# Exponentials drawn together ahead of a sine, and a later place for the values' loads and sums

## The chip, the cores and the metric

The kernel runs on one core of a Trainium2 chip. A core has five engines with their own instruction queues: TensorE (PE, whose weight loads are listed as PEld), VectorE (DVE), ScalarE (ACT), GpSimd (POOL) and SyncE (SP), which here issues almost all DMA transfers. Each engine works through its queue in order and waits at semaphores for the others. The metric is the device time of one execution in microseconds (us); lower is better. A single execution with the hardware profiler gives the trace; its times are counted from the first instruction of the span.

## The reference

An attention with pooled keys and values is followed by a two-layer network with a snake activation, all in float32:

```python
B, H, S, D = 8, 8, 576, 64
k_p = k.reshape(B, H, S // 8, 8, D).mean(axis=3)      # 72 pooled keys per head
v_p = v.reshape(B, H, S // 8, 8, D).mean(axis=3)
scores = np.matmul(q, k_p.transpose(0, 1, 3, 2)) / np.sqrt(D)
attn = np.exp(scores - np.max(scores, axis=-1, keepdims=True))
attn = attn / (np.sum(attn, axis=-1, keepdims=True) + 1e-09)
x = np.matmul(attn, v_p)              # -> (4608, 512), heads side by side
h = x @ w_in                          # 512 -> 2048
s = np.sin(alpha * h)
g = h + s * s / (alpha + 1e-09)
out = g @ w_out                       # 2048 -> 512
```

## The kernel before

The network's first layer runs over the 4608 rows in nine units of 512 (`u` = 0 to 8), and each unit in four groups (`J` = 0 to 3) of the 2048 columns. The products use a scheme of seven block products in place of eight, so a group consists of seven products. They are the seven steps `k` = 0 to 6 of a group, and a unit thus has 28 *slots* (slot = 7 J + k). `hidden` writes this order out by hand. For each slot it records the copies, sines and squares of the group on ScalarE, the additions on VectorE, then whatever is listed for the slot in `extra`, and then the slot's product on TensorE (L833). Since every engine works through its queue in the order of recording, the slot of a piece of work fixes what it stands behind.

`carry` makes the list `extra` of each unit. While unit `u` is multiplied, the attention of batch `b = u + 1` is worked in between, for the 512 rows that the next unit needs. Its steps, with their lines in the profile, are these:
- `load_v` (L141, L146): six DMA transfers on SP bring the values into the tiles `kvin` (two of 512 KB) and `vr` (four of 64 KB). `pool_main` adds the values of `kvin` up into `vm` on GpSimd in three additions (L132), and `pool_v` those of `vr` into `vz` in four (L132 and L152).
- `load_k` (L122), twice per unit: each call brings 576 KB of the keys of the batch after the next into a `kvin` tile; `pool_k` adds each up on GpSimd (L132) into `kp`. The `kvin` tiles come from a pool of two buffers, so that the three loads of a unit take turns: the second key load uses the buffer that the unit's values were in.
- `load_q` (L85, L106): the queries of the unit after the next.
- `two_scores` (L309 on TensorE, L332 and L333 on VectorE): the scores of four row tiles, less their maximum, into `ex`.
- `exp` (L358, ScalarE) on each of the four tiles, 128x864 the last one and 128x576 the others; `norm`: sum and reciprocal on VectorE (L364, L365), then the multiplication by it on GpSimd (L366), called the division here.
- `turn` (L492 to L502): block transposes on VectorE into the tile `tr`; `move` (L512): 16 DMA transfers on SP from `tr` into `aM`.
- `all_values` (L601, L614): the products with the values, and the copies (L528) that write the next unit's rows.
- `turn_q` (L220, L225 on VectorE, L235 on SP): the queries are transposed in the same way, through the same buffer `tr`, and moved.

Four things of `hidden` matter beside these. In steps 1 and 3 of a group ScalarE copies one PSUM bank into another (L811) before the next product may add to it. In step 4 the group's first sine comes (L980), followed by its square (L987). Groups 1 to 3 of the units 1 to 6 take one product from seven smaller ones (L962; group 3 a second one, L1010); their raw results are copied by ScalarE (L967) and added on GpSimd (L795, five additions, the *raw sums*, recorded in step 2). And the finished `g` of a group is written to DRAM by SP (`store_g`, L1046).

Sine and exponential need different function tables on ScalarE: where one follows the other, the program has a table load (ACT_TABLE_LOAD).

The units 1 to 6 are those that run the part of `carry` that the diff touches; unit 6 has no keys and no queries to load any more. When unit 8 is done, the second layer (L1310) runs alone to the end.

In the code of `hidden` the extras of step 4 stand behind the sine and the square:

```python
            elif k == 4:
                ...
                    sin(G, 0, 0, G.b1)
                    square(G, 0, 0)
                extras()
                ...
                product(G, 7, G.b7, part=(0, 1))
```

Of the kernel before, what the change touches and what calls it, by code (L numbers as in the profile page):

```python
# [41 lines left out]
class Kernel:  # L42
# [1107 lines left out]
    def carry(self, u):  # L1150

        nc = self.nc
        x = defaultdict(list)
        at = lambda slot, f, *a: x[slot].append(lambda: f(*a))
        last = self.B - 1
        b = u + 1
        if u == 0:
            A0, A = self.att[:2]
            at(1, self.sum_v_rows, 0, 1, 2)
            at(1, A0.rest_q)  # L1160
            at(1, A0.a_head, 1, (5, 7, 2))
            at(2, A0.values, (2, 3), (2, 1), 1, 1)
            at(2, A0.score, 4)
            at(2, self.sums_of_x, 0, 2)
            at(2, self.sums_of_x, 0, 3)
            at(2, self.load_w_in_part, 2)
            at(2, self.load_w_in_part, 3)
            at(2, self.pairs_q, 1, range(5))
            at(4, self.combine_w_in, 1, (0, 1, 2, 3), self.nc.gpsimd)
            at(4, A.q_t, 0, self.nc.vector.tensor_copy)  # L1170
            at(4, A.q_t, 1, self.nc.vector.tensor_copy)
            at(4, A.k_t)
            at(7, self.load_v, 1)
            at(7, lambda: self.pool_main())
            at(7, lambda: self.pool_v())
            for i in range(2):
                at((5, 10)[i], A.two_scores, i)
            at(13, A.two_shifts)
            for i in range(2, 5):
                at(5 + i, A.q_t, i)  # L1180
            at(9, A0.exp, 4)
            for i in range(4):
                at((9, 9, 15, 15)[i], A.exp, i)
                at((10, 10, 16, 16)[i], A.norm, i)
                at((13, 13, 17, 19)[i], A.turn, i)
            at(8, self.combine_w_in, 2, (0, 1, 2, 3), self.nc.gpsimd)
            at(13, A0.norm_rest)
            at(17, self.combine_w_in, 3, (0, 1), self.nc.gpsimd)
            at(17, self.combine_w_in, 3, (2, 3), self.nc.gpsimd)
            at(23, A0.a_rest)  # L1190
            at(24, lambda: A0.values_rest((5, 6, 7, (self.turn + 1) % 5)))
            for r in (32, 96):
                at(3, self.nc.gpsimd.memset, self.aM[r:r + 32, :, 704:736], 0.0)
            at(19, A.move, range(3))
            at(20, A.move, (3,), nc.scalar, (0,))
            at(21, A.move, (3,), nc.scalar, (1,))
            at(26, A.all_values)
            at(9, self.load_q, 2)
            at(23, self.inner_w_in)
            for e in range(2):  # L1200
                at(12, self.load_k, 2, e)
                at(17, lambda e=e: self.pool_k[e]())
            at(27, self.att[2].k_t)
            turn = 23
        else:
            at(0, self.sums_of_x, u, 2)
            at(0, self.sums_of_x, u, 3)
        if 0 < u < last:
            A = self.att[b]
            for i in range(2):  # L1210
                at((3, 5)[i], A.two_scores, i)
            at(6, A.two_shifts)
            for i in range(4):
                at((8, 10, 10, 11)[i], A.exp, i)
                at((9, 10, 11, 12)[i], A.norm, i)
                at((12, 13, 13, 13)[i], A.turn, i)
            at(14, A.move, range(4))
            at(2, self.load_v, b)
            at(5, lambda: self.pool_main())
            at(6, lambda: self.pool_v())  # L1220
            for i in range(2):
                if b < last:
                    at(12, self.load_k, b + 1, i)
                    at(17, lambda i=i: self.pool_k[i]())
            at(25, A.all_values)
            if b < last:
                at(26, self.att[b + 1].k_t)
            if 2 < u + 2 <= last:
                at(7, self.load_q, u + 2)
            at(2, self.inner_x, u)  # L1230
            turn = 22
        elif u:
            turn = None
        if turn and u + 2 <= last:
            for part in range(4):
                at(((turn, turn + 1) if u == 0 else (23, 24))[part] if part < 2 else turn + part, self.turn_q, u + 2, part)
        if u + 1 < self.NU:
            at(27, self.sums_of_x, u + 1, 0)
            at(27, self.sums_of_x, u + 1, 1)
        return x  # L1240
# [337 lines left out]
```

## Time and profile before

| | |
|---|---|
| median of 3 runs | 922.52 us (920.09 to 923.7) |
| the profiled execution | 925.12 us |
| its span, first to last instruction | 923.3 us |
| granted TensorE clock, mean | 0.998 |
| first layer with attention, about | 0 to 528 us |
| one unit with attention, e.g. from the first scores of u=2 to those of u=3 | 150.35 to 207.66 us: 57.3 us |
| second layer alone | from 558 us to the end |
| ACT_TABLE_LOAD | 31 x 1283 ns |

The lines of the trace read as: start in us, duration in us, engine, source line, operation, the tile written and the tile read with their sizes, how many instructions were merged into the line (x2), and in brackets the idle time of the engine before it with what ended that idle time. An engine that is busy all the time can be sped up only by taking work from it; one that waits shows in the brackets for whom. For TensorE the weight loads (PEld) run ahead of the products, so a wait shows there first and a little longer.

### The profile page before, as it was taken

Reading aid. Unit: us, or ns where it says so; the run is one execution under the profiler, and the core shown is the slowest. Engines: PE = TensorE matmul, PEld = TensorE weight load, DVE = VectorE, ACT = ScalarE, POOL = GpSimd, SP = SyncE. Lnnn points to the kernel's source line nnn. Section 1 sums busy time; section 2 is a strip of 40 time slices with the busy share of each in tenths; the row PEclk is TensorE's granted clock in tenths of the full one; section 3 lists DMA queues with packets and bytes.
Section 4 is the critical chain, followed back from the end, with each engine's and each line's share of the span. In section 5 each row is a group of like instructions: output and inputs, shape, how many; then the busy total and the mean of one; then the engine's idle time right before and its main releaser. Section 6 shows DMA issues by size and latency. Waiting matters only on the chain.

```text
span 923.3 us, 18073 instructions
## 1 busy us (share of the span) xinstructions
PE 901.2 (98%) x7050; PEld 816.9 (88%) x7050; DVE 670.0 (73%) x999; ACT 462.3 (50%) x1064; POOL 264.4 (29%) x306
## 2 busy tenths in 40 slices
PE   8999999999999989999999999999999999999998
PEld 5787878788787878878888899999999999999998
DVE  7685766656566555764466989988888897989795
ACT  5686776977859758687786631111111211111111
POOL 4688663755637647463000000000000000000000
PEclk9999999999999999999999999999999999999999
DMA  9965847658466565637526237161526353443501
GB/s 255 242 195 159 244 121 204 173 155 258 127 192 180 155 208 154 169 108 212 217 92 207 103 124 222 36 219 39 181 77 170 89 159 99 135 123 99 158 15 39
DMA packets 128748, 141.14 MB, mean 153 GB/s; under 512 B 46920, under 2 KB 95704, under 8 KB 128664
## 3 DMA queue, kind: packets, MB, share of 16 engines
q1 hardware_dynamic: 125880, 137.88, 51.2%
q10 hardware_dynamic: 2784, 2.11, 0.9%
q8 instruction: 56, 0.92, 0.5%
q14 instruction: 28, 0.23, 0.1%
HBM read 75.37 MB, written 47.19 MB: 133 GB/s over the span
## 4 chain that ended last, share of the span: by engine, by line
PE 86%; ACT 10%; DVE 2%; issue 1%; POOL 1%; DVEq 0%; POOLq 0%
PE PS L1310 40%; PE PS L833 36%; PE PS L309 2%; ACT s L980 2%; PE PS L601 2%; ACT L980 2%; ACT L358 2%; ACT ex L358 2%; ACT s L987 1%; PE PS L962 1%; PE PS L1010 1%; PE PS L614 1%; ACT PS L811 1%; ACT raw L967 1%; DVE x L1265 1%
## 5 line engine op out<-in xcount | busy, mean ns | idle before, releaser
L833 PE MATMUL PS<-home,a 128*128 128x256 f32 x1104 | 257.9, 382 | 1.5 <-DVE h L810 0.7
L833 PEld LDWEIGHTS PS<-home,a 128*128 128x128 f32 x1104 | 207.1, 190 | 37.6 <-issue 5.0
L833 PE MATMUL PS<-home,as 128*128 128x256 f32 x720 | 171.6, 383 | 10.8 <-ACT PS L811 10.8
L833 PEld LDWEIGHTS PS<-home,as 128*128 128x128 f32 x720 | 133.6, 191 | 29.8 <-ACT PS L811 12.0
L1360 POOL TENSOR_TENSOR cc<-cc,cb 128x576 f32<-128x576 f32 x1 | 2.0, 1980 | 484.5 <-DVE cb L1265 484.5
L1310 PE MATMUL PS<-s,wb 128*128 128x144 f32 x896 | 119.1, 286 | 0.0
L1310 PEld LDWEIGHTS PS<-s,wb 128*128 128x128 f32 x896 | 113.7, 190 | 0.1
L987 ACT ACTIVATE s<-s,c 128x256 f32<-128x256 f32 (+1 forms) x228 | 113.4, 564 | 0.0
L810 DVE TENSOR_TENSOR h<-PS,p 128x512 f32<-128x512 f32 x72 | 49.3, 684 | 82.0 <-PE PS L833 40.7
L980 ACT ACTIVATE s<-h,al 128x256 f32<-128x256 f32 x144 | 65.0, 508 | 44.9 <-DVE h L810 44.8
L1438 ACT COPY PS<-PS 128x144 f32<-128x144 f32 x56 | 14.7, 263 | 145.0 <-PE PS L1310 138.4
L132 POOL TENSOR_TENSOR kvin<-kvin 96x768 f32<-96x768 f32 (+3 forms) x42 | 65.5, 1560 | 49.5 <-DMA kvin<-in_v_dram 47.9
L1310 PE MATMUL PS<-r,wb 128*128 128x144 f32 x512 | 73.3, 286 | 0.3 <-DVE r L1265 0.3
L1310 PE MATMUL PS<-s,a 128*128 128x144 f32 x512 | 73.2, 286 | 0.0
L980 ACT ACTIVATE s<-PS,al 128x256 f32<-128x256 f32 x144 | 59.9, 467 | 21.2 <-PE PS L833 20.2
L1310 PEld LDWEIGHTS PS<-r,wb 128*128 128x128 f32 x512 | 67.1, 190 | 0.5 <-DVE r L1265 0.5
L1310 PEld LDWEIGHTS PS<-s,a 128*128 128x128 f32 x512 | 67.1, 190 | 0.0
L1032 DVE TENSOR_TENSOR h<-PS,s 128x512 f32<-128x512 f32 x36 | 24.6, 684 | 55.1 <-ACT s L987 55.1
L811 ACT COPY PS<-PS 128x512 f32<-128x512 f32 x72 | 41.7, 579 | 37.0 <-PE PS L833 26.8
L1458 ACT COPY PS<-PS 128x144 f32<-128x144 f32 x56 | 14.7, 263 | 87.8 <-PE PS L1310 87.8
L1310 PE MATMUL PS<-s,we 128*128 128x144 f32 x384 | 54.9, 286 | 0.0
L1310 PE MATMUL PS<-x,wb 128*128 128x144 f32 x384 | 54.9, 286 | 0.0
(221 smaller groups left out, 1496.5 us busy)
## 6 DMA issues: line engine op xcount, KB each, us to landing
g_bridge<-h SPq DMA_DIRECT2D x72, 512.0 KB
r<-g_bridge SPq DMA_DIRECT2D x31, 1152.0 KB
out_dram<-o SPq DMA_DIRECT2D x122, 72.0 KB
kvin<-in_k_dram SPq DMA_DIRECT2D x14, 576.0 KB
q<-in_q_dram SPq DMA_DIRECT2D x7, 1024.0 KB
kvin<-in_v_dram SPq DMA_DIRECT2D x14, 512.0 KB
aM<-tr SPq DMA_DIRECT2D x54, 92.0 KB
aM<-tr SPq DMA_DIRECT2D x54, 88.0 KB
```

The costliest lines, as they stand in the source:

```text
L132: self.nc.gpsimd.tensor_tensor(out=t[..., 0:w] if w > D else out, in0=t[..., 0:w], in1=t[..., w:2 * w], op=OP.add)
L309: nc.tensor.matmul(ps[e][r0 + r:r0 + r + q.shape[-1], h, :], q[s], kb[s, hp, :], start=True, stop=True)
L358: nc.scalar.activation(out=E(i), in_=E(i), func=AF.Exp, scale=scale)
L601: nc.tensor.matmul(o[r:r + 64], w, x, start=start and i < 2, stop=False, skip_group_check=True)
L810: add = lambda o, x, y: nc.vector.tensor_tensor(out=o, in0=x, in1=y, op=OP.add)
L811: copy = lambda o, x: nc.scalar.copy(out=o, in_=x)
L833: nc.tensor.matmul(ps[:, jj, :], self.A[p][:, kk, f * P:(f + 1) * P], x[:, kk, :], start=(start and n == 0), stop=(kk == 1), skip_group_ch ...
L980: self.nc.scalar.activation(out=G.s[:, i, jj, j, :], in_=src[:, jj], func=AF.Sin, scale=self.al[:, f:f + 1])
L987: self.nc.scalar.activation(out=x, in_=x, func=AF.Square, scale=self.c[:, f:f + 1])
L1032: add = lambda o, x, y: self.nc.vector.tensor_tensor(out=o, in0=x, in1=y, op=OP.add)
L1310: nc.tensor.matmul(out, W[:, J // 2, J % 2, :], A[:, J, :], start=(start and J == 0), stop=(J == self.NJ - 1), skip_group_check=True)
L1438: nc.scalar.copy(out=x1[:, 0, :], in_=x0[:, 1, :])
```

## The change

Three things are moved in `carry`, for the units 1 to 6. No arithmetic is changed.

```diff
             for i in range(4):
-                at((8, 10, 10, 11)[i], A.exp, i)
+                at((8, 8, 10, 10)[i], A.exp, i)
                 at((9, 10, 11, 12)[i], A.norm, i)
                 at((12, 13, 13, 13)[i], A.turn, i)
             at(14, A.move, range(4))
-            at(2, self.load_v, b)
-            at(5, lambda: self.pool_main())
-            at(6, lambda: self.pool_v())
+            at(6, self.load_v, b)
+            at(13, lambda: self.pool_main())
+            at(17, lambda: self.pool_v())
             for i in range(2):
                 if b < last:
                     at(12, self.load_k, b + 1, i)
                     at(17, lambda i=i: self.pool_k[i]())
```

- The second exponential goes from slot 10 to slot 8, and the fourth from slot 11 to slot 10. Slot 11 is step 4 of group 1, so all four exponentials now stand ahead of that group's first sine. The program has 12 table loads fewer.
- The values are asked for in slot 6 instead of slot 2. On SP the six transfers stand behind the store of slot 6 and ahead of the queries' load of slot 7; before, they stood ahead of that store.
- The main values are added up in slot 13 instead of slot 5: on GpSimd behind the four divisions of the slots 9 to 12. The rest of the values is added in slot 17 instead of slot 6: behind the raw sums of group 2 (slot 16) and ahead of the keys' sums.

The order of the other instructions on each engine is the same as before.

## The prediction

> **What bounds the kernel now.** I first read the page's busy shares, then the weight loads' waits (they show a stalled TensorE best, since loads run ahead of matmuls), then the timeline of each engine in the unit of 199 to 258 us (u=3).
>
> ```profile
> PE 901.2 (98%) x7050; PEld 816.9 (88%) x7050; DVE 670.0 (73%) x999; ACT 462.3 (50%) x1064; POOL 264.4 (29%) x306
> PEld PS L833 <- ACT PS L811: 14.5, 12, 2.0
> ```
>
> TensorE is nearly always busy, so only its waits can be won. Twelve of them, two in each of the units 1 to 6, are for ScalarE's copy L811, 14.5 us together. ScalarE in u=3:
>
> ```profile
> 222.36 1.28 ACT L358 ACT_TABLE_LOAD   x1
> 223.66 0.68 ACT L358 ACTIVATE ex<-ex 128x576 f32<-128x576 f32 x1
> 224.25 0.95 ACT L967 COPY raw<-PS 128x512 f32<-128x512 f32 x2
> 225.08 0.60 ACT L811 COPY PS<-PS 128x512 f32<-128x512 f32 x1
> 225.60 1.26 ACT L358 ACTIVATE ex<-ex 128x576 f32<-128x576 f32 x2
> 226.88 1.28 ACT L980 ACT_TABLE_LOAD   x1
> ...
> 229.81 1.28 ACT L358 ACT_TABLE_LOAD   x1
> 231.10 0.92 ACT L358 ACTIVATE ex<-ex 128x864 f32<-128x864 f32 x1
> 232.04 1.28 ACT L980 ACT_TABLE_LOAD   x1
> ...
> 236.30 1.59 PEld L833 LDWEIGHTS PS<-home,as 128*128 128x128 f32 x8 [2.02 <-ACT PS L811]
> ```
>
> ScalarE has no gap from 222.36 to 236.25, where its copy L811 of 235.66 ends: four table loads, and the fourth exponential (x864) stands alone behind the first sine. That copy is what TensorE waits for (2.02 us by the loads, 1.83 by the matmuls). A smaller wait, 0.38 by the loads, follows the copy of 225.08.
>
> The attention's weights then travel on: exponential, sum (DVE L364), division (POOL L366), transpose (L492 to L502), move (SP L512), values (PE L601). POOL first, with the values' sums ahead of the divisions:
>
> ```profile
> 216.09 3.71 POOL L132 TENSOR_TENSOR kvin<-kvin 128x1024 f32<-128x1024 f32 x2 [6.93 <-DMA kvin<-in_v_dram]
> ...
> 227.86 3.36 POOL L366 TENSOR_TENSOR ex<-ex,sm 128x576 f32<-128x576 f32 x3
> 233.53 1.63 POOL L366 TENSOR_TENSOR ex<-ex,sm 128x864 f32<-128x864 f32 x1 [2.30 <-DVE sm L365]
> ```
>
> SP's queue (its columns: start, time, source line and transfer, how many):
>
> ```profile
> 225.22 2.05 SPq L122 DMA_DIRECT2D kvin<-in_k_dram  x2
> 237.41 11.16 SPq L512 DMA_DIRECT2D aM<-tr  x16
> ```
>
> VectorE, then TensorE, where the moves have landed:
>
> ```profile
> 250.21 1.25 DVE L220 STREAM_TRANSPOSE tr<-q 128x1024 f32<-128x1024 f32 x1 [4.13 <-DMA aM<-tr]
> 251.38 0.65 DVE L1032 TENSOR_TENSOR h<-PS,s 128x512 f32<-128x512 f32 x1
> ```
>
> ```profile
> 251.71 1.07 PE L601 MATMUL PS<-aM,vm 64*64 64x512 f32 x8
> 252.25 0.28 PE L601 MATMUL PS<-aM,vz 64*64 64x64 f32 x4
> ```
>
> The 16 moves end at 248.57 and have landed at 250.2, when DVE L220 may overwrite `tr`. L1032 stands behind L220 in VectorE's queue and frees the PSUM bank that the values' rest (`vz`) writes: it ends at 252.03 and TensorE goes on at 252.25. So a second chain already ends almost together with TensorE's own. L601 starts at 135.68, 193.4, 251.71, 309.7 and 371.43 in units 1 to 5, and L1032 ends at 135.98, 193.20, 252.03, 309.03 and 370.87; `vz` follows some 0.15 us behind L601 where nothing holds it. The second chain's slack is thus 0, 0.3, 0, 0.75 and 0.6 us, 1.65 in all.
>
> **The exponentials.** Order becomes: load, exp 0, exp 1, raw copies, b7 copy, exp 2, exp 3, load, sine. Two loads of 1.28 us go in each of 6 units. Exp 1 (about 0.58 us, the step between neighbours in the rows) moves ahead of the copy at 225.08, so that copy ends 0.6 later and TensorE loses 0.6 there. Exp 3 ends at 225.60 + 0.58 + 0.6 + 0.92 = 227.7 instead of 232.02. The sine and square take until 230.8; the last sine but one waits for DVE L810, which stands behind the fourth sum, at about 232.6; the copy for TensorE then runs near 234.3 to 234.9, and TensorE, 0.6 late, needs it at 234.47 + 0.6 = 235.1. The wait of 1.83 goes, 0.6 is added: 1.2 us won at this place per unit, with bounds of 0.6 (another wait of 0.6 left) and 2.2 (both waits gone).
>
> The saved loads are worth 2.57 us by the rows, since the sine starts at 228.17, right behind the load. The Trainium skill, "ScalarE: Activation LUTs", section "What ACT_TABLE_LOAD costs", adds a drain of about 1.38 us to each switch. By it two switches would be 5.3 us; the trace shows no such gap, and TensorE's wait would cap the gain either way.
>
> **The values' loads and sums.** `load_v` moves from slot 2 to 6 on SP: six DMA issues (2.14 + 2.68 us of SP) now stand behind the store of slot 6 and ahead of the q load, which waited until 215.15 anyway. Landing some 3 to 4 us later than 216 leaves over 10 us to the sums. Cost 0; if the saturated DMA delayed the keys, it would be a part of what follows. `pool_v` (1.65 + 0.61 us) moves into the slot of the key sums; with them it delays the raw sums of J=3 from 252.85 to some 255.5, and L810 needs them at 257.76. Cost 0.
>
> `pool_main` (3.71 + 0.72 us) moves behind the divisions, and this has a price. The pool of `kvin` has two buffers for three loads per unit, so the second key load reuses the values' buffer. In the changed program's instruction order that DMA, in slot 12, waits for `pool_main`'s last addition, as before; but this addition now stands behind the fourth division. SP works in order, and all 16 moves, the store behind them and q's moves (L235) stand behind the key load. In u=3 by the rows:
> - Raw copies 0.6 later: raw sums on POOL start at 225.47 and take 3.0; first division 228.44 to 229.59 (1.15).
> - VectorE: the first transposes wait for it, 229.62 to 230.5; the fourth sum 230.5 to 231.55 (1.06); the reciprocal lets POOL start 0.37 after its own start: 231.96.
> - Fourth division 1.63: 233.6. `pool_main` 4.5 with its gaps (216.09 to 220.60): 238.1.
> - Key load 1.0 (half of 2.05): the moves start at 239.1, not 237.41, though their data would be ready at about 236.2.
>
> The moves start 1.7 us later by the clock, and by the same chain (start 5.4 us behind the end of exp 3 in every unit of before) in all five units with keys, u=1 to 5. TensorE then waits at the values, where what it won in slot 16 is lost too: the unit is set by the late chain. Loss 5 x 1.7 - 1.65 slack = 6.85 us.
>
> Two additions. The key's 576 KB now lie ahead of the moves on the DMA. Two key loads kept DMA at 1.02 to 1.04 from 226 to 232, so one is about 3 us; the moves use 0.62 to 0.66 of it and would catch up most of that in 10 us. Also, DMA semaphores go round in eights: the eighth move waits for the key load, due at about the same time (243.5). Bounds 0 and 1.0 per unit; I take 0.4, nearer the lower since both come out even: 2.0. Then `pool_main` lies beside VectorE's L1032 (`h<-h,s`, 1.44). POOL's L795 takes 0.90 to 0.96 beside DVE L805 and 0.46 alone, so bounds are 0 and 0.5; I take 0, as only its last part could overlap. The skill's "SBUF — State Buffer", section "SBUF: two separate sides", speaks against the change more strongly: a GpSimd operation and a VectorE one with two SBUF inputs hold a shared port pair exclusively, and the loser waits for the whole instruction. By it up to 1.44 us would come on top in each unit, some 7 us over five.
>
> u=6 loads no keys, and keeps its 1.2. **Sum:** 6.85 + 2.0 - 1.2 = +7.65 us. The profiled execution has a span of 923.3 (925.12 with what lies around it), the runs a median of 922.52; I add the difference to the median: 930.
>
> **The rivals.**
> *A, the forecast:* the blocked moves decide; 925 to 938.
> *B, they cancel:* `pool_main` ends 1.5 us sooner (fourth sum not held up by the transposes), so the moves start near their old time. TensorE then goes on as before in five units, and only u=6 wins: -1 to +4, about 923. For it: my chain has eight links, each good to some 0.2. Against: the order of VectorE and POOL fixes them.
> *C, faster:* the key load costs the moves nothing, because POOL reaches `pool_main` by 231. Then TensorE keeps 1.2 in each of 6 units, -7.2, up to -11 with both waits gone: 911.5 to 917, say 915. It decides from a moves' start before 236.2. For it: four loads become two on a gapless ScalarE. Against: the fourth division alone starts after 231.
> *D, worse:* the port and the DMA at their upper bounds (5 x 0.5 and 5 x 1.0 instead of 2.0) and q's moves late for the next scores (L309 starts at 207.66, 2.4 us behind the end of their issue at 205.27; both shift with the values, so only a further delay shows): 936 to 945.
>
> **How the numbers follow.** A 0.60, B 0.21, C 0.14, D 0.05. About 0.5% (4.6 us) is what a measurement of this kernel can tell from no change. Slower by more: nearly all of A and D less A's lower edge, 0.62. Faster by more: C, 0.14. Same: B and A's edge, 0.24. The range 917 to 938 leaves out C's larger part and D; A alone spans 925 to 938.
>
> **What would show it.** SP's second L122 would start near the end of `pool_main`, 12 to 13 us behind the first; L512 would start some 1.7 us later against TensorE's slot 8; the L811 wait of 2.02 would be gone and one of 0.38 grown to about 1.0; L601 would wait 2 to 3 us for DMA `aM<-tr` or DVE L1032 in units 1 to 5, not in 6. If L122's second issue comes by 235, or L601 shows no wait, the step with the key load is wrong, and the time falls below 920.

## The result and the profile after

The changed kernel takes 935.18 us (median of 4 runs, 933.51 to 936.21). The kernel before takes 922.07 us (4 runs, 920.09 to 923.70). The ratio is 1.0141, with an interval of 1.0116 to 1.0167, so the change costs about 13 us. The profiled execution after has a span of 933.9 us, the one before had 923.3. The forecast was 930 with a range of 917 to 938: the sign and the mechanism were right, and the loss was put too low, at 8 instead of 13 us.

First the page after, with its busy shares and the chain that ended last (shares of the span by engine):

```profile
PE 909.7 (97%) x7050; PEld 817.4 (88%) x7050; DVE 667.3 (71%) x999; ACT 446.7 (48%) x1052; POOL 258.5 (28%) x306
...
PE 65%; ACT 3%; DVE 3%; DMA 3%; SPq 2%; POOL 1%; issue 1%; DVEq 0%; POOLq 0%
```

In the chain before, PE had 86% and ACT 10%, and neither DMA nor SP's queue (SPq) had a share. ScalarE has its 12 loads less, 15.6 us of busy time (462.3 before), and nearly left the chain; DMA and SP's queue entered it. (The shares listed do not add up to 100%.) The waits of the weight loads after (line, releaser: total us, times, longest) begin with

```profile
PEld PS L601 <- DVE h L1032: 8.3, 5, 1.9
PEld PS L601 <- POOL raw L795: 6.2, 3, 2.3
PEld PS L833 <- ACT PS L811: 5.7, 6, 0.9
```

The 14.5 us for L811 of before became 5.7. New are the waits at L601, the products with the values, and they are longer than what was saved. The second line names GpSimd; the timeline of the products, further down, puts the same waits down to the moves (`aM<-tr`). SP's own waits show where those were held:

```profile
SPq L122 <- POOL vm L132: 62.9, 5, 12.8
```

Five times, once per unit with keys, the second key load waits up to 12.8 us for the last addition of `pool_main`. The same unit as in the prediction (u=3) lies 7.5 us later in the new trace. ScalarE there:

```profile
233.15 0.60 ACT L811 COPY PS<-PS 128x512 f32<-128x512 f32 x1
233.67 1.50 ACT L358 ACTIVATE ex<-ex 128x576 f32<-128x576 f32 x2
235.19 1.28 ACT L980 ACT_TABLE_LOAD   x1
```

The fourth exponential ends at 235.17. Counted from the start of the copy L811 shown above it that is 2.0 us, where before (225.08 to 232.02) it was 6.9. What follows on GpSimd and on SP:

```profile
235.93 5.08 POOL L366 TENSOR_TENSOR ex<-ex,sm 128x576 f32<-128x576 f32 x4
240.97 3.72 POOL L132 TENSOR_TENSOR kvin<-kvin 128x1024 f32<-128x1024 f32 x2
244.77 1.65 POOL L132 TENSOR_TENSOR vm<-kvin 128x256 f32<-128x256 f32 x1
```

```profile
232.72 14.06 SPq L122 DMA_DIRECT2D kvin<-in_k_dram  x2
246.88 10.96 SPq L512 DMA_DIRECT2D aM<-tr  x16
```

The divisions end at 241.0, but the moves, which carry the divided weights, start at 246.88, when the additions have ended at 246.42. The two key loads fill 14.06 us of SP instead of 2.05. TensorE gets there at 257.84:

```profile
259.49 1.08 PE L601 MATMUL PS<-aM,vm 64*64 64x512 f32 x4 [1.65 <-DMA aM<-tr]
261.36 0.33 PE L601 MATMUL PS<-aM,vm 64*64 64x64 f32 x4 [0.79 <-DVE h L1032]
261.52 0.28 PE L601 MATMUL PS<-aM,vz 64*64 64x64 f32 x4
...
264.86 1.61 PE L614 MATMUL PS<-aM,vz 32*128 32x512 f32 x8
```

It waits for the moves to land, issues four products, and waits again for L1032. VectorE shows why: L220, which waits for the same moves since it overwrites `tr`, stands ahead of the L1032 that TensorE needs, the last of these lines. (The first line is an earlier L1032, which comes up again with the prediction.)

```profile
244.62 1.22 DVE L1032 TENSOR_TENSOR h<-h,s 128x1024 f32<-128x1024 f32 x1
...
259.48 1.25 DVE L220 STREAM_TRANSPOSE tr<-q 128x1024 f32<-128x1024 f32 x1 [7.33 <-DMA aM<-tr]
260.65 0.65 DVE L1032 TENSOR_TENSOR h<-PS,s 128x512 f32<-128x512 f32 x1
```

One more loss came unforeseen. The table by stretches of this trace (stretch, its length, busy time and instructions of PE, PEld, DVE, ACT, POOL, then TensorE's granted clock, DMA share and GB/s):

```profile
260.00:262.00 2.00, 1.21 (x24) 0.65 (x24) 2.00 (x3) 0.00 (x0) 1.59 (x3) 1.00 0.90 339
262.00:264.00 2.00, 2.00 (x30) 1.04 (x22) 2.00 (x3) 0.90 (x3) 0.00 (x0) 0.61 0.01 4
264.00:266.00 2.00, 2.00 (x12) 0.52 (x8) 0.14 (x1) 0.00 (x0) 0.00 (x0) 0.54 0.55 131
266.00:268.00 2.00, 2.00 (x15) 1.44 (x8) 0.00 (x0) 1.50 (x6) 0.00 (x0) 1.00 0.40 98
```

Behind the two waits TensorE is fully busy from 262 to 266, but the granted clock is only 0.61 and 0.54. So the values' own products take longer too.

Where the 13 us come from is seen when each unit is counted from the start of its L811 copy in slot 8 (220.53 before and 228.03 after in u=3). "Behind the copy" means this below. The values' rest is the first product with `vz`. The times, in us, are read from the timelines of both traces in the six units:

| event, units 1 to 6 | before | after |
|---|---|---|
| the moves start | 16.90 16.88 16.88 16.88 16.88 16.92 | 18.86 18.85 18.85 18.84 18.84 15.26 |
| values' rest on TensorE | 31.71 31.35 31.72 31.35 31.35 31.36 | 33.52 33.56 33.49 33.84 32.82 29.92 |
| first product behind the values | 34.95 34.59 35.05 34.59 34.59 34.59 | 38.45 38.44 38.37 38.72 36.08 33.15 |

The moves are 1.97 us later in each of five units, the rest of the values 9.75 us in all (1.81 + 2.21 + 1.77 + 2.49 + 1.47), and unit 6, without keys, wins 1.44. From the rest to the next product it took 3.23 to 3.33 us before; after, 4.88 to 4.93 in the units 1 to 4 and 3.26 in unit 5: another 6.54. Together that is 9.75 - 1.44 + 6.54 = 14.85 us.

The medians differ by 13.1 and the profiled spans by 10.6. Part of the gap to 14.85 lies between the units, from this next product to the next unit's copy: there the profiled execution of before lost 5.4 us more than the one after. Its TensorE waited twice among the scores (L309) for something that the profile does not name, 0.75 us in u=3 and 2.45 us in u=5, and behind the second wait its granted clock was 0.50 for a while too. From the trace of before, a product and a stretch:

```profile
332.44 0.71 PE L309 MATMUL PS<-kblk,q 64*64 64x72 f32 x26 [2.45 <-issue]
334.00:336.00 2.00, 2.00 (x6) 1.56 (x6) 0.00 (x0) 0.00 (x0) 1.92 (x3) 0.50 0.81 260
```

This does not look like mere chance. In the profiled executions of the six kernels that load the values in slot 2, before among them, the longest such wait of the weight loads at L309 is 0.3, 0.4, 1.8, 2.3, 2.6 and 2.8 us; in the six that load them in slot 6, after among them, it is 0.3 us each time. So the later `load_v` may save some time of its own. No run tests it alone, and what the products wait for there stays open.

### The profile page after: what moved, and what is told of

Same layout as the page of the kernel before. It is cut to its first block, busy times and chain, and to the rows that moved or that the text cites. A ratio compares the mean times of both kernels' runs of the same rounds, so it can differ in the third digit from the quotient of the medians.

```text
span 933.9 us, 18049 instructions
## 1 busy us (share of the span) xinstructions
PE 909.7 (97%) x7050; PEld 817.4 (88%) x7050; DVE 667.3 (71%) x999; ACT 446.7 (48%) x1052; POOL 258.5 (28%) x306
## 4 chain that ended last, share of the span: by engine, by line
PE 65%; ACT 3%; DVE 3%; DMA 3%; SPq 2%; POOL 1%; issue 1%; DVEq 0%; POOLq 0%
PE PS L1310 40%; PE PS L833 21%; PE PS L601 2%; SPq L512 2%; DMA kvin<-in_k_dram 2%; PE PS L309 1%; ACT s L987 1%; DMA aM<-tr 1%; PE PS L614 1%; ACT raw L967 1%; DVE x L1265 1%; DMA g_bridge<-h 1%; POOL vm L132 1%; POOL p L795 0%; ACT s L980 0%
## 5 line engine op out<-in xcount | busy, mean ns | idle before, releaser
L810 DVE TENSOR_TENSOR h<-PS,p 128x512 f32<-128x512 f32 x72 | 49.3, 685 | 90.2 <-PE PS L833 32.3
L1032 DVE TENSOR_TENSOR h<-PS,s 128x512 f32<-128x512 f32 x36 | 24.6, 684 | 53.4 <-ACT s L987 53.4
L811 ACT COPY PS<-PS 128x512 f32<-128x512 f32 x72 | 41.7, 579 | 35.2 <-PE PS L833 26.9
```

What stands on the lines that cost most here:

```text
L810: add = lambda o, x, y: nc.vector.tensor_tensor(out=o, in0=x, in1=y, op=OP.add)
L811: copy = lambda o, x: nc.scalar.copy(out=o, in_=x)
L1032: add = lambda o, x, y: self.nc.vector.tensor_tensor(out=o, in0=x, in1=y, op=OP.add)
```

## The experiments

"After" is the changed kernel. Each result has the kernel before beside it, on the same chip (medians 923.30 or 923.52).

**One part alone: the exponentials.** The kernel before with the new places of the exponentials only.

```diff
-                at((8, 10, 10, 11)[i], A.exp, i)
+                at((8, 8, 10, 10)[i], A.exp, i)
```

> Exponentials alone in their new slots, the values' loads and sums as before the change. Theory (the second key load, held by the values' main sums, blocks the moves on SP): that block is absent here, so the moves start some 1.3 us earlier than before the change, TensorE keeps about 1.4 us in each of the units 1 to 6, and the time is 914 (911 to 917). Rival 1 (the exponentials themselves cost, by the copy they push back in slot 10): 922 or more. Rival 2 (the values' chain ends no sooner anyway, nothing is won): 919 to 923.

Measured: 914.11 us, ratio 0.9897 [0.9862, 0.9932]. The weight loads' waits for L811 fall as in the changed kernel, from twelve of 14.5 us in all to six of 5.7, and the time by about 9 us. By itself this part is a gain.

**The other part alone: the values.** After, with the exponentials put back to the slots 8, 10, 10, 11.

> Values' loads and sums alone in their new slots, the exponentials as before the change. Theory: the fourth division ends at its old, later time, so the main sums behind it hold the second key load some 3.5 us beyond the old start of the moves in the units 1 to 5, TensorE's wait in slot 16 stays, and its clock drops after the waits at the values: 940 to 946. Rival 1 (the exponentials' new slots are what costs): 922 or less. Rival 2 (the late loads of the values cost through the saturated DMA, a fixed price): 931 to 936, without longer waits at L601 than in the changed kernel.

Measured: 937.29 us, ratio 1.0149 [1.0106, 1.0191]. The whole loss is in the values' part, and against after (935.18) the new exponentials bring only 2 us. The expected 940 to 946 was too high: the moves start 2.7 us later than before (19.57 behind the copy instead of 16.88), not 3.5, and the products behind the values were slowed in the units 2 and 3 alone (4.9 us from the rest to the next product, 3.24 in the other three units). GpSimd's last addition was not held up here:

```profile
245.96 0.73 POOL L132 TENSOR_TENSOR vm<-kvin 128x256 f32<-128x256 f32 x1
```

The one that waited was VectorE's L1032 beside it:

```profile
246.01 1.76 DVE L1032 TENSOR_TENSOR h<-h,s 128x1024 f32<-128x1024 f32 x1
```

It had started 0.05 us later. In after L1032 started first (244.62) and kept its 1.22 us, while `vm` (244.77) took 1.65.

**One line of the values' part.** The first experiment's kernel, with `pool_main` alone moved to slot 13; load and rest stay in their old slots.

```diff
-            at(5, lambda: self.pool_main())
+            at(13, lambda: self.pool_main())
```

> The exponentials in their new slots, and of the values' work only the main sums moved to slot 13; the values are loaded in slot 2 and the rest is summed in slot 6 as before the change. Theory (the main sums alone hold the second key load and so the moves): all of the loss is there, 932 to 937, with the second key load on SP ending 12 to 13 us behind the first and waits at L601 in the units 1 to 5. Rival (the later loads of the values or the later sums of their rest carry a good part): 914 to 928.

Measured: 936.78 us, ratio 1.0148 [1.0120, 1.0176], the ratio of after within the intervals. The moves start 18.85 to 18.87 behind the copy, as in after, and SP's L122 waits for `vm` again, up to 12.8 us and 65.1 in all.

This one line costs 22.7 us (914.11 to 936.78, runs from two chips). The later `load_v` and `pool_v` cost nothing that can be measured (936.78 without them, 935.18 with them).

**The same line put back differently.** After, with `pool_main` in slot 8 instead of 13: behind the landing of the late values, ahead of the divisions.

```diff
-            at(13, lambda: self.pool_main())
+            at(8, lambda: self.pool_main())
```

> The changed kernel with the main sums in slot 8, ahead of the divisions; the values' loads stay in slot 6 and the sums of their rest in slot 17. Theory: the values have landed by then, the second key load goes out at once, no wait at L601, and the time is near that of the exponentials alone (914.1): 913 to 918. Rival (loads in slot 6 and sums in slot 17 cost by themselves): 922 or more.

Measured: 914.90 us, ratio 0.9910 [0.9888, 0.9932]. SP's queue around the moves:

```profile
223.04 2.24 SPq L122 DMA_DIRECT2D kvin<-in_k_dram  x2
234.23 10.75 SPq L512 DMA_DIRECT2D aM<-tr  x16
```

The two key loads again take 2.24 us, and the exponentials' gain is back.

**The late additions kept, the key load out of the way.** After, with only the second key load behind the moves (slot 15).

```diff
-                    at(12, self.load_k, b + 1, i)
+                    at((12, 15)[i], self.load_k, b + 1, i)
```

> The changed kernel with one edit: the second key load is issued in slot 15, behind the 16 moves on SP, instead of slot 12. Theory: nothing holds the moves any more, L601 does not wait, the keys still land before GpSimd comes to them, and the time is that of the exponentials alone, 914 (911 to 918). Rival (the later sums on GpSimd, or the later value loads, cost by themselves): 924 or more, with waits for POOL or DVE left in the units 1 to 5.

Measured: 921.35 us, ratio 0.9972 [0.9949, 0.9995], and not the 914 that I expected. SP does what was meant:

```profile
236.56 10.62 SPq L512 DMA_DIRECT2D aM<-tr  x16
247.28 0.52 SPq L122 DMA_DIRECT2D kvin<-in_k_dram  x1
```

The moves no longer stand behind a wait, and the waits at L601 went with it. But the key is now asked for at 247.28 and GpSimd wants it long before it has landed:

```profile
252.63 3.72 POOL L132 TENSOR_TENSOR kvin<-kvin 96x768 f32<-96x768 f32 x2 [4.12 <-DMA kvin<-in_k_dram]
```

Behind these key sums stand the raw sums of the last group; VectorE's L810 waits 6.41 us for those, and TensorE waits for L810:

```profile
PEld PS L833 <- DVE h L810: 11.5, 12, 1.9
```

I had moved a load and not asked who waits for it.

**The same with the key sums later.** In addition, the second key sum goes from slot 17 to slot 24, behind those raw sums.

```diff
-                    at(17, lambda i=i: self.pool_k[i]())
+                    at((17, 24)[i], lambda i=i: self.pool_k[i]())
```

> The kernel with the second key load behind the moves, and that load's sums in slot 24, behind the fourth group's raw sums, instead of slot 17. In the run before, GpSimd waited 4.1 us for that load ahead of those raw sums, VectorE's L810 for them and TensorE 1.9 us for L810. Theory: that is all that was left of the loss; the waits for DVE L810 and POOL kp go, 913 to 917. Rival (something else of the values' move costs): 920 or more.

Measured: 914.17 us, ratio 0.9901 [0.9878, 0.9924]. The moves start 15.23 behind the copy in the units 1 to 5, as with the exponentials alone (15.23 to 15.41). Of the 11.5 us for L810, 1.4 are left, and 4.8 us of waits appear at products that read the late key sums (L270, for `kp`).

`pool_main` stands behind the divisions as in after, and the time is that of the exponentials alone. The late additions as such thus cost nothing in sum; the key load that waits for them, in front of the moves, costs it all. A third `kvin` buffer, which should take the wait away without any other move, was not tried.

**The clock alone.** After, with products into an unused bank put around the first products of the values in the units 1 to 5, so that TensorE has work while it waits. Nothing else is earlier.

```diff
+            fills = 1 < b < self.B - 1
+            if fills:
+                self.keep_busy(7)
...
+            if fills:
+                self.keep_busy(4)
...
+    def keep_busy(self, n):
+        for _ in range(n):
+            self.nc.tensor.matmul(self.psum([P, 4, P], 7), self.full[:],
+                self.full[:].unsqueeze(1).to_broadcast([P, 4, P]), start=True, stop=True)
```

> The changed kernel with 7 bf16 products into an unused PSUM bank ahead of the values' first product and 4 more behind it, in the units 1 to 5, so that TensorE is busy while it waits; the waits themselves stay. Theory that the waits make the granted clock drop for some 3 us (0.54 to 0.61 at 262 to 266 us in the changed kernel): the drop goes, the values' products take 2.3 us from the rest on as before the change, and the time falls by some 1.2 us in four units, 929 to 932. Rival (the drop has another cause, or the products only lengthen the wait): 935 or more, with the low clock still there.

Measured: 928.85 us, ratio 1.0054 [1.0033, 1.0075]. The timeline of TensorE (L1257 is the filling; the lines below it moved by five, so that L619 is L614):

```profile
254.87 1.67 PE L1257 MATMUL PS<-full 128*128 128x512 bf16 x7
256.47 1.08 PE L601 MATMUL PS<-aM,vm 64*64 64x512 f32 x4
257.48 1.04 PE L1257 MATMUL PS<-full 128*128 128x512 bf16 x4
258.45 0.33 PE L601 MATMUL PS<-aM,vm 64*64 64x64 f32 x4
...
260.78 1.14 PE L619 MATMUL PS<-aM,vz 32*128 32x512 f32 x8
```

The stretches behind it, columns as above:

```profile
258.00:260.00 2.00, 2.00 (x37) 1.06 (x39) 2.00 (x3) 0.82 (x3) 0.87 (x2) 1.00 0.17 52
260.00:262.00 2.00, 2.00 (x27) 0.72 (x20) 0.57 (x1) 0.14 (x2) 0.00 (x0) 1.00 0.31 72
```

The clock stays at 1.00 and the products of L614's line take 1.14 us instead of 1.61. From the rest of the values to the next product it is 3.24 us in every one of the units 1 to 5, as before the change, instead of 4.88 to 4.93 in four of them. The rest itself comes no earlier than in after (33.41 to 34.01 behind the copy, where after had 32.82 to 33.84). Useless work brought 6.3 us by the medians (8 us by the ratios), close to the 6.54 lost behind the rest and a little more than expected: the granted clock, not only the wait, was part of the loss.

**A better version.** The copy of slot 10, which TensorE needs in slot 11, had become 0.6 us later by the second exponential, and that is the wait of 5.7 us that the exponentials alone left. Here only the fourth exponential moves, in the kernel before:

```diff
-                at((8, 10, 10, 11)[i], A.exp, i)
+                at((8, 10, 10, 10)[i], A.exp, i)
```

> The exponentials alone moved, but the second to slot 10 too (slots 8, 10, 10, 10), so that it no longer stands ahead of the copy that TensorE needs in slot 11. Theory (that copy is on TensorE's path, the second exponential costs 0.55 us there): the waits for L811 fall from 5.7 to some 2.3 us, no new one in slot 16, 911 (908 to 913). Rival (ScalarE's work then ends later in front of slot 16 and the wait returns there): 914 or more.

Measured: 910.44 us, ratio 0.9868 [0.9843, 0.9893], and the waits shrink again:

```profile
PEld PS L833 <- ACT PS L811: 2.3, 6, 0.4
```

Since this lies close to 914.11 and was run on another chip, both were run once more on one chip, first the exponentials of the change and then this one.

> The exponentials alone in the change's new slots once more, on one chip with the next kernel, since the intervals of the two overlap. Theory: ratio to the kernel before 0.990 (0.988 to 0.992).

> The exponentials alone in the slots 8, 10, 10, 10 once more. Theory (the second exponential ahead of slot 11's copy costs about 0.55 us in six units): ratio to the kernel before 0.9865 (0.985 to 0.988), 3 us below the kernel beside it. Rival (no difference beyond run to run): within 1.5 us of it.

Measured: 913.98 us, 0.9913 [0.9882, 0.9944], and 911.49 us, 0.9878 [0.9846, 0.9909]. Both are faster than the kernel before. That the second is the better by 2.5 us is indicated twice and fits the waits, but the intervals overlap.

## Why the prediction was right, and where it fell short

**The second key load blocks the moves: right, and shown.** Taking it from the front of the moves (with its sums out of the way) or letting `pool_main` end early each brings the time from 935 to 914. Counted on the clock of before (less 7.5 us), the fourth exponential ends at 227.67 (forecast 227.7), the first division starts at 228.43 (228.44), the fourth division ends at 233.5 (233.6) and `pool_main` at 238.92 (238.1).

**The moves 1.7 us later: 1.97.** Two small terms were off, in opposite directions. The last addition took 1.65 us instead of 0.72, beside VectorE's L1032; I had taken nothing for this, with the argument that only its last part could overlap, and the last part is what the key load waits for. The term lies between my bound of 0.5 and the skill's rule: by "SBUF — State Buffer", section "SBUF: two separate sides", the loser waits for the whole other instruction, and the 0.93 us here, as the 1.76 instead of 1.22 of L1032 in the second experiment, agree with it to 0.14 us (both end that much sooner than a full wait gives). The key load itself, on the other hand, held SP for less than 0.5 us instead of 1.0 (`vm` ended at 246.42, the moves started at 246.88).

**The key's bytes ahead of the moves, 2.0 us: about 1.15.** From the start of the moves to their landing (the start of L220) it took 61.63 us before and 62.78 after, over the five units. Unit 4 has 1.14 of the difference, so it is no fixed price per unit, and that the key's bytes cause it is not shown. The slack was 1.2 us and not 1.65: where it waits, the rest follows the end of L1032 by some 0.2 us (252.03 and 252.25 in the prediction's unit), which the forecast left out. Delay of the values' rest in all: 9.8 + 1.15 - 1.2 = 9.75, forecast 8.5 + 2.0 - 1.65 = 8.85. The sum came near because its terms were off in both directions, which was luck.

**The exponentials' gain lost in five of six units: right.** They bring about 9 us alone and 2 us in the changed kernel. Unit 6 keeps 1.44 (forecast 1.2). In size, 9 us over six units is 1.5 us each, within the bounds of 0.6 to 2.2. The drain of 1.38 us per switch, which the prediction quoted from the skill, shows nowhere: behind a load of 1.28 us the next activation starts at once (235.19, then 236.48 after).

**What the sum lacked: the clock.** The prediction ended each unit at the values' rest and took what follows as unchanged. It was some 1.6 us longer in four units, 6.54 us in all, over four tenths of the 14.85. I had the granted clock of before (0.998) in the table and didn't ask what a wait of 2 to 3 us would do to it, though the trace of before showed what it can do: the clock of 0.50 behind the wait of 2.45 us, at 334 us. That is the step that failed, and for the most part it is why 935 came and not 930. That 935 lies inside the stated range is owed to the range's width. A corrected sum, 9.75 - 1.44 + 6.54 on a median of 922.5, gives some 937; the waits of before at L309, which after does not have, may be the rest.

**The rivals.** *C* gave 915 if the key load cost the moves nothing. Two kernels that meet this condition take 914.17 and 914.90, so its price was right and its condition false in the changed kernel. *B* fell with the moves' start. *D* (936 to 945) lay near in time, but not by its causes: the later landing cost 1.15 us where it needed 5.0 for the DMA, and the port's price is in the moves' start. Without the clock's 6.54 us the rest, 9.75 - 1.44 = 8.3, would have given some 931, well inside *A*.

**`load_v` and `pool_v` at nothing: right,** by the kernel that left both in place and took the same time within the intervals.

## What to carry to other kernels

When work that frees a buffer is moved later, look for the transfer that waits for this buffer and for everything queued behind that transfer on its issuing engine: here a harmless addition on an idle engine cost 22.7 us through a queue in which it doesn't appear. A wait that moves between engines is costed to the end of the unit, with the clock after it, and not just to the point where the engine goes on. And before a load is moved out of the way, ask who waits for its data, as the kernel with the key behind the moves shows.

## What the hardware showed unexpectedly

In the trace of after the granted clock fell to 0.50 four times, for 3.41 us each time, from 139.56, 201.00, 262.44 and 323.88 us on. These starts are 61.44 us apart, 18 times 3.413, though the units' copies of slot 8 are 61.18 to 61.31 us apart: the drops keep to a grid of their own. In every other trace here that has a drop, its start and end lie on such a grid too. Half the clock for 3.41 us is 1.7 us of a busy TensorE's work, and 1.55 to 1.69 us is what each of the four units lost.

Each drop came behind a stretch in which TensorE had only four products, of about 1.08 us together: 3.52 (135.49 to 139.01), 3.58, 3.52 and 3.87 us long in the units 1 to 4 of after. In unit 5 the stretch was 2.84 us and the clock stayed at 1.00; in the kernel with the values' part alone, stretches of 2.96 and 2.75 us were followed by a clock of 0.50, and so were two of its six plain waits of about 1.8 us for L811 in slot 16, while the same waits of before were not. So no length of wait separates the cases. The idle time in the 3.41 us just ahead of a drop doesn't either (1.25 us at the one of 262.44; twice 1.83 without a drop in the values' kernel), and what exactly sets off the drop stays open. The Trainium skill, "TensorE: Matmul & The Clock Gate", section "Part 1: The HAM clock gate (the "warmup" mystery)", tells of a clock that halves after an idle window of about 3.4 us, counted by a free-running window, and comes back after as much sustained work. The free-running window fits the grid, and the 3.41 us at half clock agree; an engine that is quite idle for 3.4 us isn't needed here, since the four products lay inside each stretch. Eleven cheap products per unit were enough to hold the clock, at 0.999 or 1.000 in all 12 executions, against 0.990 to 0.993 in the four of after.
